# Chunked attention and two feed-forward layers: sums on GpSimd, decode order, side-work edges and rotating output banks

## The chip, the cores and the metric

One core of a Trainium2 chip. It has TensorE (PE; matmuls and, beside them, weight loads, PEld), VectorE (DVE), ScalarE (ACT), GpSimd (POOL) and SyncE (SP), which mostly issues DMAs. Each engine takes its own instructions in order and waits on semaphores. Matmuls write PSUM, here eight banks of 128 x 512 fp32. The metric is the device time of one execution in microseconds.

## The reference

The four weight matrices arrive as float64, the other inputs as fp32. The kernel decodes each weight into an fp32 value from the two 32-bit words of its float64.

```
attention: q, k, v of (8, 8, 576, 64); in each chunk of 64 rows
           softmax(q k^T / 8) v, sums + 1e-9
x = the result as (4608, 512)
h = x @ w_in (512 x 2048);  g = s * relu(h)^2 + b;  y = g @ w_out (2048 x 512)
h2 = y @ w2_in;             g2 = h2 * sigmoid(1.702 h2);  out = g2 @ w2_out
```

## The kernel before, in words

**Tiling.** The 4608 tokens are nine blocks (j) of 512. The 2048 hidden columns are 16 tiles (i) of 128. Every fp32 operand is kept as a rounded part and a rest (hi and lo), and a product is three matmuls: lo x hi, hi x hi, hi x lo. One matmul of 128 x 128 by 128 x 512 fills one bank.

**First layer, blocks 2 to 8 ("steady tiles").** `gemm_in` makes one hidden tile in 12 matmuls into one of two h banks (L487). Then ACT takes Relu (L499) into a buffer r, DVE squares and scales (L500), ACT adds b and rounds to gh (L501), DVE makes the rest gl (L502). Two tiles later `gemm_out` multiplies gh, gl by the second weights into four banks acc0 to acc3 (L562). Blocks 0 and 1 are done at the start, with hidden tiles kept as squares while the weights are still being decoded. Buffers named r, p, qt, kt, pt, wm, wc, ost and so on are all taken from one pool of ten (`tmp`).

**Decoding (`decode`, L116 to L132).** A weight arrives as pairs of 32-bit words (high, low). ACT brings down the low word's upper bits into c (L120), DVE shifts and joins exponent and fraction (L121, L124), GpSimd adds c (L128), ACT squares the high word as fp32 (L129), DVE multiplies by a mask that zeroes tiny values (L131). First weights are then split by ACT (L146) and DVE (L147). Each yield ends a step of the plan; at the start two weights are in flight.

**Second weights and their sums.** While blocks 2 to 8 run, each second weight is decoded and written to DRAM by a GpSimd DMA (L177). `sums` then reads four quarters of two weights back (L190), forms sums and differences for a seven-product block multiplication (Strassen's scheme in Winograd's form) on GpSimd (L193 to L196), rounds them in an ACT copy (L198), takes the rest on GpSimd (L199) and stores both parts by SyncE DMAs (L204). There are 32 such sums, 64 stores of 448 KB.

**Second layer.** Block 0 runs as in the first layer. Blocks 1 to 8 run as four pairs (`Halves`). First phase: eight hidden steps i, each of seven products M1 to M7 (L658) into a bank "x" (acc0 to acc3 by i mod 4), a bank "d" and a bank "b". ACT keeps partial results (L666); `quarter` adds them (L677), takes the sigmoid (L679) and multiplies (L680). M7 and M4 reuse the bank x: M4 may start when quarter 22 has been read by L677, and the bank is free when quarter 21 has been read by L680. Second phase: seven output products in the order M1, M5, M6, M2, M7, M3, M4, each over the eight i and two sides z (L753), with x banks acc2 and acc3; operands are split by ACT and DVE (L730, L731). `result` adds (L769), transposes (L772) and stores four strips by SyncE DMAs (L776).

**Order.** The work is a list of items with planned times (`at`, in units of which a steady tile takes two). It is traced in that order, and a scheduler with a simulated timeline then sets the order on each engine: an instruction whose buffer is not free lets later ones pass. `IN_ORDER` edges bind the order of two instructions of one engine without a semaphore. Items added by `steps_at` are called `step`: attention, decoding, sums and the operands of x.

Of the kernel before, what the change touches and what calls it, by code (L numbers as in the profile page):

```python
# [44 lines left out]
def chunk_attention_two_ffn(ctx, tc, q, k, v, w1_in, w1_out, s, b, w2_in, w2_out, out):  # L45
# [70 lines left out]
    def decode(st, m, c):  # L116

        high, low = st[:, :, 1], st[:, :, 0]
        t = m.bitcast(I32)
        nc.scalar.activation(out=c.bitcast(I32), in_=low.bitcast(U32), func=AF.Copy, scale=2.0 ** -29)  # L120
        nc.vector.tensor_scalar(  # L121
            out=t, in0=high, scalar1=3, scalar2=0x3FFFFFF8, op0=ALU.logical_shift_left, op1=ALU.bitwise_and
        )
        nc.vector.scalar_tensor_tensor(  # L124
            out=t, in0=high, scalar=-0x40000000, in1=t, op0=ALU.bitwise_and, op1=ALU.bitwise_or
        )
        yield
        nc.gpsimd.tensor_tensor(out=t, in0=t, in1=c.bitcast(I32), op=ALU.add)  # L128
        nc.scalar.activation(out=c, in_=high.bitcast(F32), func=AF.Square)  # L129
        yield  # L130
        nc.vector.scalar_tensor_tensor(out=m, in0=c, scalar=TINY * TINY, in1=m, op0=ALU.is_ge, op1=ALU.mult)  # L131
        yield  # L132
# [51 lines left out]
    def sums(kind, i, z):  # L184
# [13 lines left out]
        nc.scalar.activation(out=hi, in_=q[:, 1:8, :], func=AF.Copy)  # L198
# [4 lines left out]
        for part, src in enumerate((hi.bitcast(F32), q[:, 1:8, :])):  # L203
            nc.sync.dma_start(out=to[:, :, part, :], in_=src)  # L204
# [274 lines left out]
    def gemm_in(f, j, i):  # L479
        n = sizes[j]  # L480
        hi, lo = W[f, "wi", i]
        assert done[f, j] == KD
        ps = h_ps.tile([P, n], F32, tag="h", name="h")
# [14 lines left out]
        if f == 0:  # L498
            nc.scalar.activation(out=r, in_=ps, func=AF.Relu)  # L499
            nc.vector.scalar_tensor_tensor(out=r, in0=r, scalar=s_ap, in1=r, op0=ALU.mult, op1=ALU.mult)  # L500
            nc.scalar.activation(out=gh, in_=r, func=AF.Identity, bias=b_ap)  # L501
            nc.vector.scalar_tensor_tensor(  # L502
                out=gl, in0=r, scalar=b_ap, in1=gh.bitcast(F32), op0=ALU.add, op1=ALU.subtract
            )
        else:
            nc.scalar.activation(out=r, in_=ps, func=AF.Sigmoid, scale=1.702)
            nc.vector.tensor_tensor(out=r, in0=ps, in1=r, op=ALU.mult)
            split(gh, gl, r)
# [76 lines left out]
    class Halves:  # L585


        def __init__(self, j, base):
            self.j, self.base = j, base
            self.x, self.w, self.g, self.op, self.ps, self.kept = {}, {}, {}, {}, {}, {}  # L590
# [57 lines left out]
        def first(self, i, m):  # L648
            key = i, BANK[m]
            start = key not in self.ps  # L650
            if start:
                self.bank(key, BANK[m], f"acc{i % KD}")
# [89 lines left out]
        def second(self, n, i):  # L742
            m = OUT_ORDER[n]
            hi, lo = self.op.pop((n, i))
            w = self.wo[n, i // 2]
            for z in range(2):
                key = "out", z, BANK[m]
                start = m in ("M1", "M5", "M2")
                if start and i == 0:
                    self.bank(key, BANK[m], f"acc{HK + z}")  # L750
# [30 lines left out]
        def plan_second(self):  # L781
            self.wo = {}
            base = self.base + 3.5 * HF
            for n, m in enumerate(OUT_ORDER):
                for r in range(HF // 2):
                    at(base + 4 * n + r - 9, self.load_wo, n, r)
                for i in range(HF):
                    t = base + 4 * n + 0.5 * i
                    at(t - 3, self.operand, n, i)
                    at(t, self.second, n, i)  # L790
                done = base + 4 * n + 4.1
                for z in range(2):
                    if m in ("M1", "M5", "M6"):
                        at(done, self.keep_out, z, BANK[m], {"M6": "M16"}.get(m, m))
                    else:
                        at(done, self.result, {"M2": "11", "M7": "22", "M3": "12", "M4": "21"}[m], z)
# [85 lines left out]
    for p in range(NBLK // 2):  # L882
        Halves(1 + 2 * p, NS * (NBLK + 1) + 2 * LAG + 56 * p).plan()
    traced, last = nc.cur_bb.bb.instructions, None
    for t, _, f, a in sorted(ITEMS, key=lambda e: e[:2]):
        n = len(traced)
        f(*a)
        for ins in traced[n:] if t < 2 * NS else ():
# [28 lines left out]
```

## Time and profile before

| | |
|---|---|
| median of 3 runs | 1657.01 us (1655.79 to 1657.5) |
| profiled execution: time, span | 1660.28 us, 1658.5 us |
| PE busy | 1604.2 us (97%) |
| VectorE, ScalarE, GpSimd busy | 1149.3, 747.0, 266.9 us |
| mean granted clock of TensorE | 0.99 |
| HBM traffic | 163 GB/s over the span |

The stages, by the trace: the start with blocks 0 and 1 lasts to about 265 us, blocks 2 to 8 to about 870, block 0 of the second layer to about 1028, and the four pairs take 155 us each. A matmul's end is modelled, so busy time of PE says where it had work, not how well it used the time. "L487 <- ACT r L499" is read as: an instruction of line 487 stood until ACT's instruction of line 499 on buffer r had finished. The number in brackets behind a timeline row is the idle time of the engine just before it.

### The profile page before, as it was taken

The page shows a single profiled execution, that of the slowest core. Times are in us where ns is not written, and L with a number is a line of the kernel's source. Part 1 is how long each engine was busy: PE and PEld are TensorE (multiplying, and loading weights), DVE is VectorE, ACT ScalarE, POOL GpSimd, SP SyncE. Part 2 cuts the span into 40 slices and gives each one's busy share as a digit, 9 for nine tenths or more (in the row PEclk, how much of TensorE's full clock was granted, in tenths as well). Part 3 has the DMA queues.
Part 4 walks back from the last instruction along what each step waited for, and adds up shares of the span by engine and source line. Part 5 has one row for each costly group of instructions (what it writes and reads, how often), then busy time and mean ns, then how long its engine had stood idle before and what let it go on. Part 6 is the DMA issues. An engine that isn't in the chain of part 4 may idle for free.

```text
span 1658.5 us, 24595 instructions
## 1 busy us (share of the span) xinstructions
PE 1604.2 (97%) x8928; PEld 1312.8 (79%) x8928; DVE 1149.3 (69%) x1836; ACT 747.0 (45%) x1258; POOL 266.9 (16%) x294
## 2 busy tenths in 40 slices
PE   6879999999999999999999999999999999999998
PEld 5758887778788878888888888878887888788876
DVE  5876666867687775777757543579568946984685
ACT  3768543333333333333345532456345525653552
POOL 1322101333223223233333000000001000100000
PEclk9889999999999999999999999999999999999999
DMA  9435445656455554646456441676868686767654
GB/s 229 114 102 162 121 132 131 146 132 163 122 141 145 143 136 132 156 128 155 117 160 216 135 135 45 188 239 221 206 195 266 181 221 207 255 183 218 219 192 77
DMA packets 398345, 272.19 MB, mean 164 GB/s; under 512 B 255376, under 2 KB 345488, under 8 KB 398224
## 3 DMA queue, kind: packets, MB, share of 16 engines
q1 hardware_dynamic: 390800, 249.64, 55.0%
q0 software_dynamic: 5120, 16.78, 3.0%
q10 hardware_dynamic: 2304, 4.20, 0.7%
q8 instruction: 71, 1.16, 0.3%
q14 instruction: 50, 0.41, 0.1%
HBM read 209.72 MB, written 60.82 MB: 163 GB/s over the span
## 4 chain that ended last, share of the span: by engine, by line
PE 77%; DVE 8%; DMA 4%; SPq 3%; ACT 3%; issue 2%; POOL 2%; POOLq 0%; DVEq 0%; ACTq 0%
PE acc L562 19%; PE h L487 18%; PE x L658 11%; PE x L753 11%; PE d L658 5%; PE d L753 5%; PE b L658 3%; PE b L753 3%; SPq L235 2%; PE sc L287 1%; PE xT L271 1%; DVE gl L502 1%; DVE r L500 1%; DVE pt L261 1%; ACT gh L501 1%
## 5 line engine op out<-in xcount | busy, mean ns | idle before, releaser
L487 PE MATMUL h<-xh,wi 128*128 128x512 f32 x1280 | 402.7, 396 | 13.5 <-ACT r L517 5.4
L562 PE MATMUL acc<-gh,wo 128*128 128x512 f32 x1152 | 354.8, 394 | 6.0 <-ACT gh L96 3.7
L487 PEld LDWEIGHTS h<-xh,wi 128*128 128x128 f32 x1280 | 240.3, 190 | 66.3 <-ACT r L517 6.3
L562 PEld LDWEIGHTS acc<-gh,wo 128*128 128x128 f32 x1152 | 215.5, 189 | 53.0 <-ACT gh L96 4.1
L487 PE MATMUL h<-xl,wi 128*128 128x512 f32 x640 | 251.2, 394 | 0.0
L562 PE MATMUL acc<-gl,wo 128*128 128x512 f32 x576 | 220.3, 392 | 3.8 <-DVE gl L502 3.8
L501 ACT ACTIVATE gh<-r,sb 128x512 fp32r<-128x512 f32 x112 | 80.9, 723 | 184.4 <-DVE r L500 184.1
L500 DVE SCALAR_TENSOR_TENSOR r<-r,sb 128x512 f32<-128x512 f32 x112 | 103.9, 928 | 64.3 <-ACT r L499 63.8
L502 DVE SCALAR_TENSOR_TENSOR gl<-r,sb,gh 128x512 fp32r<-128x512 f32 x112 | 107.3, 959 | 57.2 <-ACT gh L501 57.1
L487 PEld LDWEIGHTS h<-xl,wi 128*128 128x128 f32 x640 | 121.7, 190 | 25.9
L562 PEld LDWEIGHTS acc<-gl,wo 128*128 128x128 f32 x576 | 108.1, 188 | 28.6 <-DVE gl L502 6.2
L128 POOL TENSOR_TENSOR wm<-wm,wc 128x512 int32<-128x512 int32 x52 | 75.7, 1459 | 338.6 <-DVE wm L124 176.9
L730 ACT ACTIVATE op<-wo 128x512 fp32r<-128x512 f32 x128 | 79.5, 630 | 79.4 <-PE d L753 25.9
L680 DVE TENSOR_TENSOR wo<-wo,r 128x512 f32<-128x512 f32 x96 | 66.0, 691 | 63.0 <-ACT r L679 62.6
L753 PE MATMUL x<-op,wi 128*128 128x512 f32 x432 | 104.4, 389 | 0.0
L658 PE MATMUL x<-xh,wi 128*128 128x512 f32 x320 | 99.5, 391 | 3.1 <-DVE wo L677 3.1
L261 DVE STREAM_TRANSPOSE pt<-p 32x256 f32<-32x256 f32 x224 | 97.7, 436 | 3.9
L597 POOL DMA_DIRECT2D xr<-y x32 | 17.3, 540 | 506.3 <-DVE op L731 262.8
L679 ACT ACTIVATE r<-wo 128x512 f32<-128x512 f32 x96 | 60.8, 633 | 76.8 <-DVE wo L677 76.0
L753 PEld LDWEIGHTS x<-op,wi 128*128 128x128 f32 x432 | 81.1, 188 | 16.9
L731 DVE TENSOR_TENSOR op<-wo,op 128x512 fp32r<-128x512 f32 x128 | 85.2, 680 | 7.4 <-ACT op L730 6.0
L198 ACT ACTIVATE wst<-wst 128x896 fp32r<-128x896 f32 x32 | 30.5, 953 | 128.1 <-POOL wst L196 83.5
(145 smaller groups left out, 2780.1 us busy)
## 6 DMA issues: line engine op xcount, KB each, us to landing
wi<-wo_sums SPq DMA_DIRECT2D x112, 512.0 KB, 3.9
wi<-wi_sums SPq DMA_DIRECT2D x96, 512.0 KB, 3.7
wst<-in_moe_w_out SPq DMA_DIRECT2D x32, 512.0 KB, 4.6
wi_sums<-wst SPq DMA_DIRECT2D x32, 448.0 KB, 3.6
wo_sums<-wst SPq DMA_DIRECT2D x32, 448.0 KB, 3.5
wst<-in_moe_w_in SPq DMA_DIRECT2D x24, 512.0 KB, 5.0
y<-ost SPq DMA_DIRECT2D x36, 256.0 KB, 3.3
xr<-y POOLq DMA_DIRECT2D x32, 256.0 KB, 6.1
```

The costliest lines, as they stand in the source:

```text
L128: nc.gpsimd.tensor_tensor(out=t, in0=t, in1=c.bitcast(I32), op=ALU.add)
L261: nc.vector.transpose(out=pt[r.start + ek * BK:r.start + (ek + 1) * BK, :, eq * BK:(eq + 1) * BK], in_=p[r.start + eq * BK:r.start + (eq + ...
L487: nc.tensor.matmul(out=ps, lhsT=w_[:, kk, :], rhs=x_, start=kk == 0 and a == 0, stop=kk == KD - 1 and a == 2,)
L500: nc.vector.scalar_tensor_tensor(out=r, in0=r, scalar=s_ap, in1=r, op0=ALU.mult, op1=ALU.mult)
L501: nc.scalar.activation(out=gh, in_=r, func=AF.Identity, bias=b_ap)
L502: nc.vector.scalar_tensor_tensor(out=gl, in0=r, scalar=b_ap, in1=gh.bitcast(F32), op0=ALU.add, op1=ALU.subtract)
L562: nc.tensor.matmul(out=acc[m], lhsT=l_, rhs=r_, start=i == 0 and a == 0, stop=i == KF - 1 and a == 2)
L658: nc.tensor.matmul(out=self.ps[key], lhsT=l_, rhs=r_, start=start and k == 0 and a == 0, stop=k == HK - 1 and a == 2, skip_group_check=not ...
L680: nc.vector.tensor_tensor(out=g, in0=h, in1=r, op=ALU.mult)
L730: nc.scalar.activation(out=hi, in_=src, func=AF.Copy)
L731: nc.vector.tensor_tensor(out=lo, in0=src, in1=hi.bitcast(F32), op=ALU.subtract)
L753: nc.tensor.matmul(out=self.ps[key], lhsT=l_, rhs=r_, start=start and i == 0 and a == 0, stop=i == HF - 1 and a == 2, skip_group_check=not ...
```

## The change

- `decode`: Square now writes the staged tile's low words instead of c and comes before the mask; the GpSimd add comes last, after the mask.
- `sums`: the rounding copy moves from ScalarE to GpSimd, and the two stores from SyncE's queue to GpSimd's.
- Steady tiles of the first layer: the four instructions behind a hidden tile are noted with a planned time, and every instruction of a `step` item gets an order-only edge behind the latest noted instruction of its own engine whose time is not later.
- `Halves`: a `turn` of 0, 2, 0, 2 for the four pairs rotates the x banks; the hidden steps begin at acc(turn), the outputs take acc(turn) and acc(turn + 1).
- In the last pair, the last product does side 0 for i = 2 to 7 before side 1, and the result of side 0 is planned right behind it.

```diff
 def decode(st, m, c):
...
         yield
+        square = low.bitcast(F32)
+        nc.scalar.activation(out=square, in_=high.bitcast(F32), func=AF.Square)
+        nc.vector.scalar_tensor_tensor(out=m, in0=square, scalar=TINY * TINY, in1=m, op0=ALU.is_ge, op1=ALU.mult)
+        yield
         nc.gpsimd.tensor_tensor(out=t, in0=t, in1=c.bitcast(I32), op=ALU.add)
-        nc.scalar.activation(out=c, in_=high.bitcast(F32), func=AF.Square)
-        yield
-        nc.vector.scalar_tensor_tensor(out=m, in0=c, scalar=TINY * TINY, in1=m, op0=ALU.is_ge, op1=ALU.mult)
         yield
 def sums(kind, i, z):
...
-        nc.scalar.activation(out=hi, in_=q[:, 1:8, :], func=AF.Copy)
+        nc.gpsimd.tensor_copy(out=hi, in_=q[:, 1:8, :])
...
-            nc.sync.dma_start(out=to[:, :, part, :], in_=src)
+            nc.gpsimd.dma_start(out=to[:, :, part, :], in_=src)
 def gemm_in(f, j, i):
...
+        def steady(d, engine):
+            served.append((NS * j + 2 * i + d, engine, nc.cur_bb.bb.instructions[-1]))
...
             nc.scalar.activation(out=r, in_=ps, func=AF.Relu)
+            steady(2, ACT)
             nc.vector.scalar_tensor_tensor(out=r, in0=r, scalar=s_ap, in1=r, op0=ALU.mult, op1=ALU.mult)
+            steady(2.2, DVE)
             nc.scalar.activation(out=gh, in_=r, func=AF.Identity, bias=b_ap)
+            steady(2.6, ACT)
...
+            steady(2.8, DVE)
 class Halves:
...
+            self.turn = j // 2 * HK % KD
...
-                self.bank(key, BANK[m], f"acc{i % KD}")
+                self.bank(key, BANK[m], f"acc{(self.turn + i) % KD}")
...
-                    self.bank(key, BANK[m], f"acc{HK + z}")
+                    self.bank(key, BANK[m], f"acc{(self.turn + z) % KD}")
...
-                    at(t, self.second, n, i)
-                done = base + 4 * n + 4.1
+                    if self.last and n == len(OUT_ORDER) - 1 and i >= 2:
+                        for z in range(2):
+                            at(base + 4 * n + 1 + 1.5 * z + 0.25 * (i - 2), self.second, n, i, (z,))
+                    else:
+                        at(t, self.second, n, i)
                 for z in range(2):
+                    done = base + 4 * n + (2.6 if self.last and n == len(OUT_ORDER) - 1 and z == 0 else 4.1)
...
     for t, _, f, a in sorted(ITEMS, key=lambda e: e[:2]):
         n = len(traced)
         f(*a)
+        for ins in traced[n:] if f.__name__ == "step" else ():
+            first = next((g for u, e, g in reversed(served) if u <= t and e == ins.engine), None)
+            if first is not None:
+                tc.add_manual_dep(ins, first.name, IN_ORDER, reason="behind the tile before")
```

## Rows read from the trace of the kernel before

**Rows 1.** The page: busy us, share of the span, instructions by engine.
```profile
PE 1604.2 (97%) x8928; PEld 1312.8 (79%) x8928; DVE 1149.3 (69%) x1836; ACT 747.0 (45%) x1258; POOL 266.9 (16%) x294
```

**Rows 2.** Busy us by stage: PE, PEld, DVE, ACT, POOL; clock, DMA share, GB/s.
```profile
40.00:80.00 40.00, 33.86 (x255) 27.38 (x254) 31.97 (x55) 28.27 (x52) 12.42 (x9) 0.87 0.49 117
80.00:120.00 40.00, 30.29 (x260) 23.07 (x261) 32.29 (x54) 26.79 (x51) 11.71 (x8) 0.87 0.31 102
...
1040.00:1195.00 155.00, 152.74 (x673) 125.79 (x672) 113.28 (x180) 76.97 (x134) 4.31 (x8) 1.00 0.72 213
```

**Rows 3.** What PE waited for, whole span: us in total, times, longest.
```profile
PE x L753 <- DVE wo L680: 5.8, 4, 1.5
...
PE x L658 <- DVE wo L677: 3.1, 4, 0.8
```

**Rows 4.** Timeline of PE at the middle of the first pair: start, length, instruction.
```profile
1100.75 0.74 PE L658 MATMUL x<-xh,wi 128*128 128x512 f32 x2 [0.79 <-DVE wo L677]
...
1111.13 0.62 PE L658 MATMUL x<-xh,wi 128*128 128x512 f32 x2
...
1114.12 0.74 PE L753 MATMUL x<-gh,wi 128*128 128x512 f32 x2 [1.47 <-DVE wo L680]
```

**Rows 5.** What PE waited for in 290 to 610 us.
```profile
PE acc L562 <- DVE gl L502: 3.8, 3, 1.4
PE h L487 <- ACT r L499: 2.2, 1, 2.2
PE acc L562 <- ACT gh L501: 1.3, 2, 0.8
```

**Rows 6.** Timeline of ACT: three of the sums' copies and the stand before each.
```profile
337.52 0.95 ACT L198 ACTIVATE wst<-wst 128x896 fp32r<-128x896 f32 x1 [9.94 <-POOL wst L196]
...
422.75 0.95 ACT L198 ACTIVATE wst<-wst 128x896 fp32r<-128x896 f32 x1 [6.60 <-DMA wo_sums<-wst]
...
591.36 0.96 ACT L198 ACTIVATE wst<-wst 128x896 fp32r<-128x896 f32 x1 [5.86 <-DMA wo_sums<-wst]
```

**Rows 7.** Busy us and clock right behind the stand that ends at 337.52.
```profile
338.00:342.00 4.00, 3.00 (x9) 2.45 (x10) 2.23 (x2) 1.67 (x3) 2.96 (x2) 0.76 0.51 131
342.00:346.00 4.00, 4.00 (x16) 3.15 (x15) 0.73 (x1) 0.58 (x1) 1.37 (x3) 0.81 0.92 245
```

**Rows 8.** Timelines of GpSimd and DVE at 338 us, and DVE at 591.
```profile
338.54 2.10 POOL L199 TENSOR_TENSOR wst<-wst 128x896 fp32r<-128x896 f32 x1 [1.06 <-ACT wst L198]
...
338.99 2.21 DVE L500 SCALAR_TENSOR_TENSOR r<-r,sb 128x512 f32<-128x512 f32 x1 [5.90 <-ACT r L499]
...
591.33 0.75 DVE L500 SCALAR_TENSOR_TENSOR r<-r,sb 128x512 f32<-128x512 f32 x1
```

**Rows 9.** Timelines of DVE and of SyncE's queue at the end.
```profile
1650.81 1.40 DVE L772 STREAM_TRANSPOSE ost<-x 128x512 f32<-128x512 f32 x2 [6.60 <-PE x L753]
...
1651.56 4.14 SPq L776 DMA_DIRECT2D out<-ost  x8
```

**Rows 10.** What PE waited for in 240 to 290 us.
```profile
PE h L487 <- ACT r L499: 2.0, 2, 1.2
```

**Rows 11.** What ACT waited for in 40 to 120 us, the rows of L129.
```profile
ACT wc L129 <- POOL wm L128: 4.2, 6, 1.4
ACT wi L129 <- POOL wi L128: 4.1, 6, 2.0
```

**Rows 12.** Groups by line: busy us, mean ns | idle before, what ended it.
```profile
L199 POOL TENSOR_TENSOR wst<-wst 128x896 fp32r<-128x896 f32 x32 | 68.1, 2129 | 50.0 <-ACT wst L198 50.0
...
L129 ACT ACTIVATE wc<-wst 128x512 f32<-128x512 f32 x52 | 34.9, 672 | 33.9 <-POOL wm L128 30.7 <-DMA wst<-in_moe_w_out 3.1
L198 ACT ACTIVATE wst<-wst 128x896 fp32r<-128x896 f32 x32 | 30.5, 953 | 128.1 <-POOL wst L196 83.5 <-DMA wo_sums<-wst 26.0 <-DMA wi_sums<-wst 11.7
...
L597 POOL DMA_DIRECT2D xr<-y x32 | 17.3, 540 | 506.3 <-DVE op L731 262.8 <-ACT r L679 136.5 <-DVE wo L147 39.1
```

**Rows 13.** Busy us of the staged tiles' own instructions, 290 to 910 us.
```profile
290.00:910.00 620.00, 0.00 (x0) 0.00 (x0) 34.47 (x60) 70.49 (x92) 138.90 (x160) 1.00 0.56 146
```

More of the change, by code (lines that the diff above doesn't have):

```diff
@@ L585, in chunk_attention_two_ffn, with __init__ @@
     class Halves:
-        def __init__(self, j, base):
-            self.j, self.base = j, base
+        def __init__(self, j, base, last):
+            self.j, self.base, self.last = j, base, last
+            self.turn = j // 2 * HK % KD
             self.x, self.w, self.g, self.op, self.ps, self.kept = {}, {}, {}, {}, {}, {}
@@ L740, in chunk_attention_two_ffn, with second @@
         n_ops = 0
-        def second(self, n, i):
+        def second(self, n, i, sides=(0, 1)):
             m = OUT_ORDER[n]
-            hi, lo = self.op.pop((n, i))
+            hi, lo = self.op[n, i]
             w = self.wo[n, i // 2]
-            for z in range(2):
+            for z in sides:
                 key = "out", z, BANK[m]
@@ L882, in chunk_attention_two_ffn @@
     for p in range(NBLK // 2):
-        Halves(1 + 2 * p, NS * (NBLK + 1) + 2 * LAG + 56 * p).plan()
+        Halves(1 + 2 * p, NS * (NBLK + 1) + 2 * LAG + 56 * p, p == NBLK // 2 - 1).plan()
+    served = []
     traced, last = nc.cur_bb.bb.instructions, None
```

## The prediction

> **What bounds the kernel now.** I read four views, from wide to narrow. The busy totals come first: TensorE (PE) is busy 97% of the span [rows 1], so a part of the change is worth what it takes out of PE's idle time, or out of the time in which PE has the slow clock. The table by stage shows where these are [rows 2]: at 40 to 120 us PE idles 6.1 and 9.7 us at a mean clock of 0.87; a stage of one pair of blocks (155 us) idles 2.26 us. PE's list of waits then names the causes. In the pair stages they are two, four times each, once per pair: 5.8 us for L680 and 3.1 us for L677 [rows 3]. In the steady tiles, 290 to 610 us, they are six waits of 7.3 us in all, for the instructions of ScalarE (ACT) and VectorE (DVE) that carry a tile from its h bank to its g operand [rows 5]. The timelines of PE and ACT show what stands behind each.
>
> **Banks by pair.** The last M4 product of a pair, from 1111.13, is followed by a gap of 1.47 us for L680, and 0.79 us is lost at 1100.75 for L677 [rows 4]. The output banks are acc2 and acc3, and the last two hidden tiles, i = 6 and i = 7, hold just these. So output side z = 1 cannot start before quarter 21 of i = 7 has been read out of its bank, and z = 0 not before i = 6 is out; PE has nothing else at hand there. With the turn, pair 0 puts its outputs in acc0 and acc1 (last held by i = 4 and 5), pair 1 in acc2 and acc3 while its hidden tiles begin at acc2, and so on. The output matmuls are then free to fill both gaps, since their operands come from quarters of earlier i. At the next pair, i = 0 and 1 take the two banks that were not outputs, and i = 2 meets the old outputs, which is where it met them before. Removed: 5.8 + 3.1 = **8.9 us**. What is late next is PE itself. Bounds: 0 if the order keeps a gap in the same place, 8.9 at most.
>
> **The end.** Now both sides of the last product end within three matmuls: two transposes from 1650.81, then eight output DMAs on SyncE's queue from 1651.56 in 4.14 us (0.52 each), to 1655.70, and the span ends at 1658.5, 2.8 us later [rows 9]. After the change side 0 ends 18 matmuls early, 4.1 us at 152.74 us for 673 [rows 2], and its transpose and four DMAs (0.7 + 2.1 us) lie beside PE. Side 1 still has its transpose (to 1652.21), then four issues (2.07) and 2.8 us: 1657.1. Gain **1.4 us**; bounds 0 (the four early DMAs come late) and 2.1 (four issues).
>
> **GpSimd alone sums.** Each of the 32 sums has an ACT copy, L198, of 0.953 us, before which ACT stood still for 128.1 us in total, 83.5 of them for GpSimd's L196 [rows 12]. ACT works in order, so a tile's Relu or bias queues behind that stand. The longest, 9.94 us, ends at 337.52; others of 6.60 and 5.86 us end at 422.75 and 591.36 [rows 6]. PE waits behind such a stand for 0.8 to 2.2 us at a time [rows 5], and I put all six waits, 7.3 us, down to L198. The 8 us from 338, right behind the longest, also ran at a mean clock of 0.76 and 0.81, that is partly at 1.2 GHz after PE's gap, which costs 4 x 0.24 + 4 x 0.19 = 1.7 us [rows 7]. Sum 9.0 us. I take **7.0 us**: L199 stays on GpSimd, and while it ran (2.10 us from 338.54) the tile's L500 took 2.21 us, where it took 0.75 at 591.33 [rows 8]; a copy by GpSimd adds a second such stretch to each sum, for which I charge 2 us. Bounds 3 and 9.
>
> The Trainium skill ("SBUF — State Buffer", Who interferes with whom) calls the port pair that GpSimd and VectorE share an exclusive lock, under which the later of the two fully blocks; this speaks against the change, and the row of 2.21 us agrees.
>
> What this part adds: 32 copies of 128x896. No row has a one-input pass of this size on GpSimd; the two-input L199 is 2.13 us, half of it is 1.06 [rows 12], and I take 1.6, between the two. Then 64 stores of 448 KB go from SyncE to GpSimd. A DMA of 256 KB holds GpSimd for 0.54 us [rows 12]; a store of the sums has seven times as many rows, shorter ones, so 0.54 to 7 x 0.54 = 3.8 us, and I take 1.0, nearest the row. GpSimd's work on staged tiles is 139 us in 290 to 910 [rows 13]; with 51 of copies, 64 of stores and some 56 of second weights (an add of 512 columns at L199's rate, 1.2 us, and a DMA, 0.54, 32 times) it is 310 of 620 us, and 506 at the upper bounds. So GpSimd stays off the path and I cost it nothing; the cover is that the sums are read only in the pair stages. SyncE loses 64 issues, and loads queued behind them go out sooner; PE's list has no wait for these, so 0.
>
> **Add last in decoding.** Before, the series of one weight is mask bits, GpSimd add, ACT Square, DVE mask, ACT copy, DVE rest; Square waits for the add because it overwrites c. Now Square goes into the staged tile's low words, beside DVE's bit work, and the add comes after the mask. The same passes remain; one Square, 0.67 us [rows 12], leaves the series. In 40 to 120 us ACT stood 4.2 + 4.1 us in front of L129 for the add, twelve times [rows 11]; that goes. But its copy L146 now waits for the add, where it waited for the mask. With two weights in flight and Squares queued behind other ACT work, most of the 0.67 us is lost again. I take **1.0 us**. Bounds: a gain of 8.3 us (all of ACT's stand comes back on PE), and a loss of 6 us (each of the twelve stands grows from its mean of 0.69 us to a whole add of 1.2).
>
> **Side work behind tiles.** These are order-only edges and add no instruction. They bind attention, second weights and sums from block 2 on. An engine must then pass the tile's instruction before that side work; if the tile is late, the side work queues behind it, and the next block's attention waits, with DVE idle 31% of the span to catch up [rows 1]. Since I put the six waits down to L198, these edges find little: 0. The two waits for Relu before 290, 2.0 us [rows 10], lie where attention steps are timed before the first tile of block 2, so they stay; if they vanish, 2.0 us more.
>
> **Sum.** 8.9 + 1.4 + 7.0 + 1.0 = 18.3 us. The profiled execution took 1660.28 us with a span of 1658.5 us: 1642.0 after. The median of the runs is 1657.01, 3.3 us less, so I put it at 1638.7, rounded to **1639 us**.
>
> **Rivals.**
>
> 1. The turn of the banks gives nothing at the turn: another wait (the read of quarter 22, or the operand split) stands where the two were. For it: L677 itself is late at 1100.75 [rows 4]. Against it: output products of side 0 ran up to 1111.13 without a gap, so operands were ready. 1638.7 + 8.9 = 1647.6. Chance 0.10.
>
> 2. Slower: GpSimd's queue becomes the late one. A decode's add follows the second sum's copy, subtraction and two stores (up to 2.1 + 2.1 + 7.6 us), and its two buffers come from the same ten from which each tile takes r. If they come back late, Relu waits. It decides once the hold outgrows 5.86 us, the shortest ACT stand of [rows 6]. 16 such places at 2.2 us, the longest wait of [rows 5]: 35 us, 1638.7 + 35 = 1674. For it: the upper bound of a store. Against it: GpSimd has half its time free. Chance 0.06.
>
> 3. Slower: the lock decides. Copy and subtraction together hold DVE for some 3.7 us at 32 places; at 1.4 us each, the longest wait for gl in [rows 5], this costs 45 us, with no gain from L198: 1638.7 + 7 + 45 = 1691. Against it: PE's waits came behind ACT stands of over 5 us, and these go. Chance 0.04.
>
> 4. The start is ordered anew for the worse: with ACT's copy behind the add, PE's idle time of 40 to 120 us (15.8 us) doubles: 1638.7 + 15.8 = 1654.5. For it: the clock of 0.87 shows how thin PE's supply is there. Against it: the same passes, one fewer in series. Chance 0.06.
>
> **Numbers.** The forecast has 0.74. Its own range: with the lower bounds of three terms and 0.7 of the first (6.2 + 0 + 3 - 6 = 3 us) 1654; with all upper bounds (8.9 + 2.1 + 9 + 8.3 + 2) 1627. Eight times in ten I expect 1629 to 1655, which holds rivals 1 and 4 too. A measurement here tells about 0.2% (3.3 us) from no change, so faster means under 1653.7: forecast and rival 1, 0.84; the same: rival 4, 0.06; slower: rivals 2 and 3, 0.10.
>
> **What would show it.** Right: L677 and L680 gone from PE's waits and pair stages of about 152.7 us; no ACT stand in front of a sum and no PE wait over 1 us in 290 to 610; four DMAs behind the last matmul; ACT's stand for the add moved from L129 to L146. Wrong: a new wait of PE on r, gl or a buffer in 290 to 910, DVE passes of 2 us in pairs, GpSimd stores above 2 us, or more idle time of PE in 40 to 120 us than 15.8 us.

## The result, and the profile after

| | before | after |
|---|---|---|
| median of 14 runs each, on the same chip | 1656.45 us (1654.48 to 1658.17) | 1664.74 us (1659.68 to 1670.54) |
| ratio, 95% interval | | 1.0054 [1.0042, 1.0065] |
| profiled execution: time, span | 1660.28, 1658.5 us | 1665.05, 1663.3 us |

The change makes the kernel 8 to 9 us slower where 18 us less were forecast; the time lies 10 us above the range. The first matmul of each stage, in us from the start of the span, says where (experiment 5 is the changed kernel with one memory doubled; experiment 1 is the kernel before with the turn of the banks alone, so up to the pairs it runs what before runs):

| | before | experiment 1 | after | experiment 5 |
|---|---|---|---|---|
| block 2, first hidden tile | 207.7 | 209.2 | 207.8 | 208.0 |
| block 3 | 365.3 | 364.2 | 358.7 | 356.9 |
| block 4 | 464.1 | 462.9 | 455.1 | 453.3 |
| block 5 | 560.6 | 559.3 | 560.8 | 550.2 |
| second layer, block 0 | 938.0 | 934.2 | 938.1 | 925.0 |
| first pair, first product of a bank x | 1035.7 | 1031.9 | 1035.8 | 1022.7 |
| end of the span | 1658.5 | 1660.4 | 1663.3 | 1651.7 |

The profiled execution of before is 3.8 us above the median of its runs, and above all 14 of them. These 3.8 us lie ahead of the pairs: experiments 1 and 2, whose engines run the same instructions in the same order up to there, both reach the first pair at 1031.9. Against experiment 1 the changed kernel is 7.8 us ahead at block 4, 1.5 us behind at block 5 and 3.9 us behind at the first pair; from there on it loses 4.7 us more against before. These are two separate losses, 8.6 us together, where the medians differ by 8.3.

By this table blocks 2 to 8 last to 938 us and block 0 of the second layer to 1036 us; the 870 and 1028 us in the section on the time before are too early.

Lines have moved in the changed kernel: L687 to L692 are the old L675 to L680, L765 is L753, L670 is L658, L678 is L666, L492 and L571 are L487 and L562, and in the first layer L504, L506, L508, L510 are Relu, square, gh, gl (L499 to L502). In decoding L129 is Square, L132 the add, L147 the split copy; of the sums L199 is the copy, L200 the rest, L205 the store; L178 stores second weights. The first line of the page (busy us, share of the span, instructions) beside [rows 1]: PE's busy time is 3.8 us longer for the same 8928 matmuls, and GpSimd's is 94 us longer.

```profile
PE 1608.0 (97%) x8928; PEld 1313.0 (79%) x8928; DVE 1172.1 (70%) x1836; ACT 719.4 (43%) x1226; POOL 360.6 (22%) x390
```

**The pairs.** What PE waited for, whole span of the changed kernel (us in total, times, longest), beside [rows 3]:

```profile
PE x L670 <- DVE wo L689: 8.7, 4, 2.2
PE acc L571 <- ACT gh L508: 7.1, 6, 3.0
...
PE x L670 <- ACT kept L678: 0.8, 4, 0.2
```

The wait for the old L680 is gone, as forecast. The one for the old L677 (now L689) has grown from 3.1 to 8.7 us, still once per pair: 9.5 us in two groups stand where 8.9 stood. PE's timeline at the middle of the first and the second pair (start, length, instruction, idle time before), beside [rows 4]:

```profile
1104.72 1.75 PE L765 MATMUL x<-op,wi 128*128 128x512 f32 x7
...
1107.67 1.97 PE L765 MATMUL x<-op,wi 128*128 128x512 f32 x8
...
1110.30 0.86 PE L670 MATMUL x<-xo,wi 128*128 128x512 f32 x3
1111.36 0.74 PE L670 MATMUL x<-xh,wi 128*128 128x512 f32 x2 [0.20 <-ACT kept L678]
...
1114.90 0.84 PE L670 MATMUL x<-xo,wi 128*128 128x512 f32 x3
1117.91 0.74 PE L670 MATMUL x<-xh,wi 128*128 128x512 f32 x2 [2.17 <-DVE wo L689]
...
1119.42 1.09 PE L765 MATMUL x<-gh,wi 128*128 128x512 f32 x4
...
1122.17 1.07 PE L765 MATMUL d<-gh,wi 128*128 128x512 f32 x4
...
1273.40 0.73 PE L670 MATMUL x<-xh,wi 128*128 128x512 f32 x2 [2.18 <-DVE wo L689]
...
1275.15 1.91 PE L765 MATMUL x<-gh,wi 128*128 128x512 f32 x4
...
1279.23 1.07 PE L765 MATMUL d<-gh,wi 128*128 128x512 f32 x4
```

From 1111.36 M6, M3, M7 (up to 1114.90) and M4 (1117.91) of i = 7 follow one another with nothing between them. M7 and M4 share the bank x, so M4 stands until DVE has read quarter 22. Before, output matmuls of side 0 stood between the two, among them these twelve:

```profile
1108.41 2.88 PE L753 MATMUL x<-op,wi 128*128 128x512 f32 x12
```

Now they have run earlier, ahead of M7 (1104.72 and 1107.67): the bank for them was free, so the scheduler took them as soon as their operands were there.

The gap is also longer than the read alone needs. DVE's read of a quarter 22 before (i = 6, the gap of 0.79 us) and in the changed kernel (i = 7):

```profile
1100.01 0.69 DVE L677 TENSOR_TENSOR wo<-x,kept 128x512 f32<-128x512 f32 x1 [0.23 <-PE x L658]
```

```profile
1117.17 0.68 DVE L689 TENSOR_TENSOR wo<-x,kept 128x512 f32<-128x512 f32 x1
```

Before, DVE stood idle for M7 and read the bank at once. Now its passes follow one another without a pause, and the read starts 1.4 us after M7's last matmul has ended (1114.90 + 0.84). So of the 2.17 us some 0.8 are the read and 1.4 are DVE's other work ahead of it; no run tests whether another order on DVE would shorten the gap. In the second pair the same four matmuls that took 1.09 us take 1.91. The table by stretch shows why (us, then busy us of PE, PEld, DVE, ACT, POOL; clock, DMA share, GB/s):

```profile
1118.00:1122.00 4.00, 4.00 (x18) 3.27 (x19) 4.00 (x8) 3.54 (x7) 0.13 (x1) 1.00 0.84 288
...
1274.00:1278.00 4.00, 4.00 (x12) 3.14 (x11) 4.00 (x7) 2.72 (x5) 0.55 (x1) 0.57 0.78 257
...
1431.00:1435.00 4.00, 4.00 (x12) 3.13 (x11) 4.00 (x8) 2.79 (x5) 0.55 (x1) 0.57 0.71 241
...
1588.00:1592.00 4.00, 4.00 (x13) 3.13 (x12) 4.00 (x8) 2.32 (x5) 0.00 (x0) 0.58 0.53 164
```

Behind the gap of 2.2 us the granted clock is 0.57 in three of four pairs, that is mostly at 1.2 GHz; behind the gaps of 1.47 and 0.79 us before, it did not fall. From M4's first matmul to the last row shown of each pair (1117.91 to 1122.17, 1273.40 to 1279.23) the same work took 4.26 and 5.83 us: 1.57 us per drop, 4.7 for three. With the 0.6 us of longer gaps and 1.4 us less at the end (run 3 below) this gives 3.9 of the 4.7 us.

**Blocks 4 and 5.** ScalarE's timeline there, then GpSimd's and PE's:

```profile
513.02 0.69 ACT L120 ACTIVATE wc<-wst 128x512 int32<-128x512 uint32 x1 [7.72 <-DMA wst<-in_moe_w_in]
...
524.65 0.68 ACT L120 ACTIVATE wc<-wst 128x512 int32<-128x512 uint32 x1 [3.95 <-DMA wst<-in_moe_w_in]
...
536.62 0.72 ACT L508 ACTIVATE gh<-r,sb 128x512 fp32r<-128x512 f32 x1 [5.84 <-DVE r L506]
```

```profile
505.47 0.91 POOL L205 DMA_DIRECT2D wo_sums<-wst  x1
...
509.37 0.91 POOL L205 DMA_DIRECT2D wo_sums<-wst  x1 [2.49 <-issue]
...
526.57 0.58 POOL L178 DMA_DIRECT2D w_wi<-wm  x1 [2.49 <-issue]
```

```profile
489.23 1.00 PE L571 MATMUL acc<-gh,wo 128*128 128x512 f32 x2 [1.85 <-ACT gh L508]
...
537.39 1.22 PE L571 MATMUL acc<-gh,wo 128*128 128x512 f32 x2 [2.96 <-ACT gh L508]
```

The groups of the sums' copy and rest on GpSimd (busy us, mean ns, then idle before), beside [rows 12]:

```profile
L200 POOL TENSOR_TENSOR wst<-wst 128x896 fp32r<-128x896 f32 x32 | 73.5, 2298 | 1.3
...
L199 POOL CAST wst<-wst 128x896 fp32r<-128x896 f32 x32 | 34.5, 1077 | 60.1 <-DMA wi_sums<-wst 31.5 <-DMA wo_sums<-wst 27.5
```

No copy of a sum is left on ScalarE, and its stands of [rows 6] are gone, but others of the same size stand there: decoding (L120) waits for its load. The load needs one of the three staging buffers. A sum takes two of them, one for the sums and one for their rounded copy, and each stays taken until the store that reads it has landed. SyncE, which issues the loads (L108), waits for that in 290 to 910 us, before and then after:

```profile
SPq L108 <- DMA wo_sums<-wst: 6.2, 8, 1.7
```

```profile
SPq L108 <- DMA wo_sums<-wst: 61.4, 10, 11.4
```

GpSimd issues a store in 0.91 us and then stands ("issue": nothing the profile shows released it) before the next DMA. At 537.39 PE waits for gh, whose DVE pass stood in a run of attention passes, and PE's gap of 2.96 us is the longest of the whole stage. With the gap of 1.85 us and a third of 0.31 PE stands 5.1 us in block 4, and behind the two long ones the clock falls:

```profile
490.00:495.00 5.00, 4.69 (x39) 3.50 (x40) 3.75 (x6) 1.63 (x3) 2.19 (x2) 0.71 0.41 96
...
535.00:540.00 5.00, 2.61 (x6) 1.82 (x7) 3.38 (x6) 1.97 (x4) 4.86 (x6) 0.73 0.07 22
```

By these rows the clock costs some 5 x 0.29 + 5 x 0.27 = 2.8 us. Together that is 7.9 of the 9.3 us by which block 4 is longer than in experiment 1 (105.7 us for 96.4).

**The start and the end.** In 40 to 120 us ACT's stand for the add has moved from L129 [rows 11] to L147 as forecast, 4.3 + 3.4 + 1.4 us for 4.2 + 4.1, and PE is busy 63.9 us of 80, as in [rows 2] (64.2). At the end side 0 is out early: DVE has one last transpose of 0.72 us where two took 1.40 [rows 9]:

```profile
1657.44 0.72 DVE L784 STREAM_TRANSPOSE ost<-x 128x512 f32<-128x512 f32 x1 [1.77 <-PE x L765]
```

### The profile page after: what moved, and what is told of

Same layout as the page of the kernel before. It is cut to its first block, busy times and chain, and to the rows that moved or that the text cites. A ratio compares the mean times of both kernels' runs of the same rounds, so it can differ in the third digit from the quotient of the medians.

```text
span 1663.3 us, 24616 instructions
## 1 busy us (share of the span) xinstructions
PE 1608.0 (97%) x8928; PEld 1313.0 (79%) x8928; DVE 1172.1 (70%) x1836; ACT 719.4 (43%) x1226; POOL 360.6 (22%) x390
## 4 chain that ended last, share of the span: by engine, by line
PE 49%; DVE 3%; ACT 0%; issue 0%
PE x L765 10%; PE x L670 9%; PE acc L571 7%; PE h L492 7%; PE d L765 5%; PE d L670 5%; PE b L765 3%; PE b L670 3%; DVE wo L592 1%; DVE op L743 1%; DVE wo L689 1%; DVE wo L692 0%; PE xT L272 0%; DVE pt L262 0%; ACT op L742 0%
## 5 line engine op out<-in xcount | busy, mean ns | idle before, releaser
L492 PE MATMUL h<-xh,wi 128*128 128x512 f32 x1280 | 401.6, 395 | 14.7 <-ACT r L526 9.4
L571 PE MATMUL acc<-gh,wo 128*128 128x512 f32 x1152 | 356.4, 394 | 7.1 <-ACT gh L508 7.1
L492 PEld LDWEIGHTS h<-xh,wi 128*128 128x128 f32 x1280 | 239.6, 189 | 66.8 <-ACT r L526 10.0
L571 PEld LDWEIGHTS acc<-gh,wo 128*128 128x128 f32 x1152 | 215.5, 189 | 54.6 <-ACT gh L508 9.6
L492 PE MATMUL h<-xl,wi 128*128 128x512 f32 x640 | 250.5, 392 | 0.0
L571 PE MATMUL acc<-gl,wo 128*128 128x512 f32 x576 | 222.5, 394 | 2.1 <-DVE gl L510 1.7
L508 ACT ACTIVATE gh<-r,sb 128x512 fp32r<-128x512 f32 x112 | 81.0, 723 | 221.6 <-DVE r L506 221.2
L506 DVE SCALAR_TENSOR_TENSOR r<-r,sb 128x512 f32<-128x512 f32 x112 | 110.6, 988 | 46.9 <-ACT r L504 46.5
L492 PEld LDWEIGHTS h<-xl,wi 128*128 128x128 f32 x640 | 121.2, 190 | 25.6
L510 DVE SCALAR_TENSOR_TENSOR gl<-r,sb,gh 128x512 fp32r<-128x512 f32 x112 | 104.8, 935 | 47.0 <-ACT gh L508 46.9
L571 PEld LDWEIGHTS acc<-gl,wo 128*128 128x128 f32 x576 | 108.3, 189 | 28.6 <-DVE gl L510 5.4
L132 POOL TENSOR_TENSOR wm<-wm,wc 128x512 int32<-128x512 int32 x52 | 77.3, 1488 | 199.5 <-DVE wm L130 187.6
L504 ACT ACTIVATE r<-h 128x512 f32<-128x512 f32 x112 | 65.8, 588 | 110.6 <-PE h L492 96.4
L692 DVE TENSOR_TENSOR wo<-wo,r 128x512 f32<-128x512 f32 x96 | 66.3, 691 | 63.3 <-ACT r L691 63.3
L670 PE MATMUL x<-xh,wi 128*128 128x512 f32 x320 | 99.8, 393 | 9.5 <-DVE wo L689 8.7
L765 PE MATMUL x<-op,wi 128*128 128x512 f32 x432 | 105.5, 389 | 0.0
L765 PEld LDWEIGHTS x<-op,wi 128*128 128x128 f32 x432 | 81.1, 188 | 16.8
```

What stands on the lines that cost most here:

```text
L492: nc.tensor.matmul(out=ps, lhsT=w_[:, kk, :], rhs=x_, start=kk == 0 and a == 0, stop=kk == KD - 1 and a == 2,)
L510: nc.vector.scalar_tensor_tensor(out=gl, in0=r, scalar=b_ap, in1=gh.bitcast(F32), op0=ALU.add, op1=ALU.subtract)
L571: nc.tensor.matmul(out=acc[m], lhsT=l_, rhs=r_, start=i == 0 and a == 0, stop=i == KF - 1 and a == 2)
L670: nc.tensor.matmul(out=self.ps[key], lhsT=l_, rhs=r_, start=start and k == 0 and a == 0, stop=k == HK - 1 and a == 2, skip_group_check=not ...
L692: nc.vector.tensor_tensor(out=g, in0=h, in1=r, op=ALU.mult)
L765: nc.tensor.matmul(out=self.ps[key], lhsT=l_, rhs=r_, start=start and i == 0 and a == 0, stop=i == HF - 1 and a == 2, skip_group_check=not ...
```

## The experiments

"Held order" below is this edit, on top of what is named: all matmuls of the first output product (n = 0) get an order-only edge, those of i = 0 behind M7 of i = 6, those of i = 1 to 7 behind M7 of i = 7.

```diff
+            if m == "M7":
+                self.m7[i] = nc.cur_bb.bb.instructions[-1]
...
+            for ins in nc.cur_bb.bb.instructions[old:] if n == 0 else ():
+                tc.add_manual_dep(ins, self.m7[HF - 1 if i else HF - 2].name, IN_ORDER, reason="kept for the turn")
```

All runs, each timed against the kernel before on its chip:

| run | median us | ratio [95%] |
|---|---|---|
| 1 before + turn | 1663.87 | 1.0046 [1.0034, 1.0058] |
| 2 before + turn + held order | 1645.91 | 0.9940 [0.9925, 0.9954] |
| 3 changed, banks as before | 1658.63 | 1.0013 [1.0001, 1.0025] |
| 4 changed + held order | 1649.33 | 0.9953 [0.9938, 0.9968] |
| 5 changed, descriptor memory 2048 | 1652.25 | 0.9976 [0.9966, 0.9985] |
| 6 = 4, descriptor memory 2048 | 1636.33 | 0.9883 [0.9866, 0.9899] |
| 7 = 4, stores on SyncE | 1632.73 | 0.9853 [0.9839, 0.9867] |
| 8 = 7, copy on ScalarE | 1634.36 | 0.9864 [0.9850, 0.9878] |
| 9 = 4, four staging buffers | 1646.39 | 0.9933 [0.9919, 0.9947] |
| 10 = 4 without edges | 1647.16 | 0.9944 [0.9930, 0.9958] |
| 11 = 7 without edges | 1632.04 | 0.9851 [0.9838, 0.9865] |
| 12 = 8 without edges | 1644.55 | 0.9921 [0.9907, 0.9935] |
| 13 = 7, decoding as before | 1638.34 | 0.9887 [0.9873, 0.9900] |

Runs 1 to 4 and 7 to 10 stood on one chip, 6 and 11 to 13 on a second, 5 on a third. Where runs on different chips are compared, the difference of the ratios is given beside that of the medians.

**1. The turn alone.** Only the three lines of `turn` on the kernel before.

> The kernel before with the rotation of the x banks alone; PE's order up to the pairs is that of before. Theory A (free output banks let the scheduler place 16 to 36 output matmuls ahead of their plan, so nothing is left to stand between the last M7 and the last M4 of a pair; one gap of 2.2 us takes the place of 1.47 + 0.79, and the clock falls behind it in most pairs): waits for L680 gone, four waits of about 2.2 us for L677, pair period 155.2 to 157.2 us, total 0 to 8 us slower than before (1.000 to 1.005). Rival B (the turn does what was forecast and the loss comes from the other parts): no PE wait at the turns, 8.9 us faster (0.9946).

It alone makes the kernel 0.46% slower, 7 us, nearly the whole loss. PE's waits and one row of its timeline:

```profile
PE x L659 <- DVE wo L678: 8.7, 4, 2.2
```

```profile
1114.00 0.73 PE L659 MATMUL x<-xh,wi 128*128 128x512 f32 x2 [2.15 <-DVE wo L678]
```

The same wait as in the changed kernel, with the sums and the decoding as before: the turn makes it. Behind it the clock falls to 0.57 or 0.58 over 4 us in three of four pairs, as expected. (L659 and L678 are here the old L658 and L677.)

**2. The turn with the order held.** Nothing is added but order edges.

> As turn_only, with order-only edges that keep the output products of i = 0 behind M7 of i = 6 and all others of the first output behind M7 of i = 7; PE then has 23 output matmuls between the last M7 and the last M4. Theory A: both waits of each pair go, pair period 152.4 to 152.9 us, no clock drop in the pairs, 8 to 9.5 us faster than before (0.9943 to 0.9952). Rival B': the banks' turn itself costs (some other wait at the turn): pair period stays 155 us or more, ratio 1.000 or above.

18 us less than run 1. Of all waits from 1020 us to the end one is left:

```profile
PE x L659 <- DMA wi<-wi_sums: 0.5, 1, 0.5
```

The stretch from the first pair's first x product to the end of the span is 612.0 us long, 622.8 before: 10.8 us less, where the forecast for the banks was 8.9 and 8 to 9.5 was expected of this run. The list of waits puts a gap at less than it costs, as these rows of the kernel before show:

```profile
1098.45 0.62 PE L658 MATMUL x<-xh,wi 128*128 128x512 f32 x2
...
1105.01 0.62 PE L658 MATMUL x<-xh,wi 128*128 128x512 f32 x2
```

The six matmuls of M7 that begin at 1098.45 and the listed 0.79 us last to 1100.75, that is 2.30 us; the next M7, from 1105.01, has its six done in 1.36, when the next matmul starts at 1106.37. So 0.94 us went there, and by [rows 4] 2.99 less 1.36, that is 1.63, at the listed 1.47. Four times both are 10.3 us. So the gap is not the price of a turn; it stands where the matmuls that could fill it have been spent.

**3. The changed kernel with the banks as before.**

```diff
-                self.bank(key, BANK[m], f"acc{(self.turn + i) % KD}")
+                self.bank(key, BANK[m], f"acc{i % KD}")
...
-                    self.bank(key, BANK[m], f"acc{(self.turn + z) % KD}")
+                    self.bank(key, BANK[m], f"acc{HK + z}")
```

> The changed kernel with the banks as before (all other parts of the change stay). Theory A: pairs like those of before (155.2 us, waits 1.47 + 0.79, no clock drop), so 5 to 7 us faster than the changed kernel and within 3 us of before: ratio 0.998 to 1.002. Rival B (the loss of the changed kernel is in the steady tiles, through GpSimd's sums or the edges): still slower than before, 1.003 to 1.006.

The old two waits are back at their old sizes:

```profile
PE x L765 <- DVE wo L692: 5.8, 4, 1.5
PE x L670 <- DVE wo L689: 3.1, 4, 0.8
```

The clock stays at 1.00 behind them in all four pairs. From the first pair to the end it takes 621.4 us for 622.8, by which the new end is worth 1.4 us (with the turn it is 1.0 us, the changed kernel against run 1, and 2.2 us, run 4 against run 2). Yet the time stays 0.13% above that of before: the sums, the decoding and the edges together cost some 3.5 us, where a gain of 8.0 was forecast. This run reaches the first pair at 1035.4, 3.5 us after run 1. Turn (+0.46%) and the rest (+0.13%) add up to the whole (+0.54%).

**4. The changed kernel with the order held.**

> The changed kernel with the same order-only edges on the first output product as turn_hold. Theory A: pair period 152.4 to 152.9 us, 14 to 16 us faster than the changed kernel; against before 8 to 12 us faster (0.9928 to 0.9952). Rival B: no better than before, 0.999 or above.

15 us less than the changed kernel (17 by the ratios), and 7.3 us under the kernel before, a little short of the 8 to 12 expected. What is left of the loss lies in 290 to 910 us: PE waits 6.4 us for gh and 1.8 for gl there.

**5 and 6. Room for GpSimd's descriptors.** The memory that the kernel sets aside for the descriptors of the DMAs that GpSimd issues is doubled; the order of the instructions on every engine stays the same. Run 6 does it on run 4, run 5 on the changed kernel itself.

```diff
-    nc = bacc.Bacc("TRN2", target_bir_lowering=False, num_devices=1, dynamic_dma_scratch_size=1024)
+    nc = bacc.Bacc("TRN2", target_bir_lowering=False, num_devices=1, dynamic_dma_scratch_size=2048)
```

> after_hold with twice the room for the descriptors of GpSimd's own DMAs (2048 in place of 1024 bytes per partition); the order of all engines is the same, instruction by instruction. Theory R (the second store of a sum stands 2.5 to 3.9 us until the first one's descriptors have been used up; this stand holds the staging buffers and delays the adds): GpSimd's stands without a visible cause before the stores and the second weights' DMAs (113 us in 290 to 910) fall below 30 us, SyncE's stands for the sums' stores below 70 us (115), PE's waits in 290 to 910 from 8 us to under 4: 3 to 10 us faster than after_hold. Rival P (a DMA issued by GpSimd stands whatever its room, or the stores land late): same stands, within 2 us of after_hold.

> The changed kernel as it is, with 2048 instead of 1024 bytes of descriptor memory for the DMAs that GpSimd issues; the order of the instructions on every engine stays. Theory (two separate causes, the emptied waits at the pairs' turns and GpSimd's full descriptor memory): the descriptor half is worth what it was worth beside the held order (1649.3 to 1636.3, so 13 us of ratio .0070), the turn half stays: 1652 to 1655 us, ratio .997 to .9995 of the kernel before; the gap of about 2.2 us before M4's first matmul stays at the pairs, with the drops of the clock behind it. Rival (the descriptor memory does it all, and the gap at the turn is worth little once the rows before it run freely): about 1640 us. Rival (the two hide each other: what the decode gains is waited for at the turn): 1662 us or more.

13.0 us (run 6 against 4; 11.6 by the ratios) and 12.5 us (run 5 against the changed kernel; 12.9 by the ratios). For run 6 that is more than the 3 to 10 us expected; run 5 lies where its first theory had it. The stores' line, L205, in the changed kernel (instructions with min, median and max ns; then the idle time before them and what ended it):

```profile
L205 POOL DMA_DIRECT2D wo_sums<-wst x32: 888/902/927, 336.7 to 921.9; - x32
...
its engine sat idle before it (us, times) until:
  issue: 78.2, 28
```

and in run 5, where no idle time is listed at all:

```profile
L205 POOL DMA_DIRECT2D wo_sums<-wst x32: 877/914/1077, 334.9 to 899.0; - x32
```

The issue itself costs the same; the 28 stands of 2.8 us on average are gone. Gone too are three stands of 9.6 us in all that the view puts down to DVE and a load, and 13 stands of 36.3 us in front of L178. ScalarE's waits for loads in 290 to 910 us, changed kernel and then run 5:

```profile
ACT wc L120 <- DMA wst<-in_moe_w_in: 25.1, 9, 7.7
ACT wc L120 <- DMA wst<-in_moe_w_out: 24.0, 7, 7.1
```

```profile
ACT wc L120 <- DMA wst<-in_moe_w_in: 13.3, 4, 4.5
...
ACT wc L120 <- DMA wst<-in_moe_w_out: 10.6, 6, 4.7
```

Both are about halved, and PE's waits in 290 to 610 us fall from 7.2 us to the 0.6 of the row below, while those at the turn stay as they were (8.7 and 0.8 us):

```profile
PE acc L571 <- DVE gl L510: 0.6, 2, 0.4
```

SyncE's waits for the sums' stores, though, only go from 115.0 us (L108 and L114 together) to 94.1 in run 5 and 93.2 in run 6, where under 70 was expected; that the staging buffers are the way by which GpSimd's stands reach PE is shown by run 9 rather than here.

In run 5 the clock falls behind the turn in all four pairs; the first of them:

```profile
1106.00:1110.00 4.00, 4.00 (x13) 3.12 (x13) 4.00 (x7) 2.00 (x4) 1.09 (x2) 0.64 0.73 258
```

So the two losses are separate and add up.

**7. The stores back on SyncE,** the copy still on GpSimd, order held.

```diff
-            nc.gpsimd.dma_start(out=to[:, :, part, :], in_=src)
+            nc.sync.dma_start(out=to[:, :, part, :], in_=src)
```

> after_hold with the 64 stores of the sums back on SyncE's queue; the rounding copy stays on GpSimd. Theory S: SyncE's stands for the sums' stores to land before a weight's load (115 us in after_hold) fall below 40 us, ACT's stand at L120 falls from 50 us to under 20, PE's waits for gh fall by 3 to 7 us, clock full after 290 us: 3 to 8 us faster than after_hold (0.990 to 0.994). Rival C (the longer chain of three passes on GpSimd, with the copy, holds the buffers): SyncE stands as long, now for L200 on GpSimd, and the time stays within 2 us of after_hold.

16.6 us less than run 4, twice what was expected, and 24 less than the kernel before: with run 11 the fastest measured. Run 6, with the stores on GpSimd but room for them, lies 3.6 us above it (5.0 by the ratios), and the intervals just touch. PE has no idle time and no slow clock in the steady tiles:

```profile
290.00:610.00 320.00, 320.00 (x2165) 263.88 (x2164) 247.76 (x390) 108.29 (x174) 124.47 (x130) 1.00 0.59 146
610.00:910.00 300.00, 300.00 (x1781) 247.76 (x1780) 217.92 (x327) 111.91 (x182) 114.42 (x120) 1.00 0.55 155
```

The Trainium skill ("DMA: Bandwidth & Descriptors", Issuing engine by pattern) gives simple loads and stores to SyncE and calls its path generally the faster one. The traces agree: an issue of 0.55 us and 3.5 us to landing on SyncE before, 0.90 us and 3.9 us on GpSimd after, beside the stands.

**8. The copy back on ScalarE as well.**

> after_hold with the copy of the sums on ACT and the stores on SyncE, as before the change. Theory S: ACT stands over 100 us in front of that copy again, and PE waits 5 to 9 us in 290 to 610 us as before; in all the time of turn_hold less 1 us at the end (ratio 0.993 to 0.995), no better than after_hold by more than 3 us. Rival C (moving the sums was a loss): 4 us or more faster than after_hold (below 0.9928).

Only 1.6 us more than run 7, and the intervals overlap: with the edges in place the copy on ScalarE costs next to nothing. The first theory, that it would bring back the old stands and 0.993 to 0.995, was wrong; the edges had been left out of it, as run 12 shows.

**9. Four staging buffers for three** (and nine tmp buffers for ten, to make room), stores on GpSimd.

```diff
-    tpool = ctx.enter_context(tc.tile_pool(name="tpool", bufs=10))
-    stpool = ctx.enter_context(tc.tile_pool(name="stpool", bufs=3))
+    tpool = ctx.enter_context(tc.tile_pool(name="tpool", bufs=9))
+    stpool = ctx.enter_context(tc.tile_pool(name="stpool", bufs=4))
```

> after_hold with four staging buffers in place of three, and nine of the shared ten buffers, for room. Theory S: a fourth buffer lets the weight's load go out before the stores have landed: SyncE's stand at L108 and L114 for the stores below 30 us, ACT's at L120 below 15, PE's waits for gh below 3 us, 3 to 8 us faster than after_hold. Rival B (r waits for one of the shared buffers): with nine of them PE's waits grow, 3 us or more slower than after_hold.

2.9 us less than run 4, intervals overlapping. Two sizes change at once, and the trace shows where each acts. Up to the first pair the run is 8.5 us ahead of run 4 (1025.1 us for 1033.6). PE's 8.2 us of waits in 290 to 910 us have shrunk to one row:

```profile
PE acc L571 <- ACT gh L508: 1.3, 1, 1.3
```

ScalarE no longer waits for a staged load there, although GpSimd still stands 86 us in front of its stores and SyncE 106.5 us for them to land (under 30 was expected). So with one staging buffer more the same stands do not reach PE: the buffers are their way. From the first pair on the run loses 9.8 us against run 4 (619.7 for 609.9), with three waits of 5.6 us in all on a buffer for kept results, which come from the pool that lost one.

**10, 11, 12. The edges behind tiles.** `add_manual_dep` is replaced by `pass`, in three settings: runs 4, 7 and 8.

> after_hold without the edges that put side work behind the tiles. Theory S (in the steady tiles GpSimd's own stores hold the staging buffers, so the next weight's load goes out late and ACT and DVE stand at L120 and L121 in front of a tile; the edges only choose where side work stands): about as after_hold, within 3 us (ratio to before 0.993 to 0.997), with ACT still standing some 50 us for staged loads. Rival E (the edges themselves make the late tiles, since side work that waits is bound in front of the next tile): PE's waits for gh fall from 7 us to under 2, 4 us or more faster than after_hold (below 0.993).

> h_sp_stores without the edges that bind side work behind tiles. Theory D (of the 12 us that h_sums_back gained over turn_hold outside the pairs, most is the decode order, since ACT no longer stands for the add): within 3 us of h_sp_stores (0.985 to 0.987). Theory E (the edges keep side work that waits from standing in front of a tile): PE waits 4 us or more in 290 to 910, 5 to 12 us slower than h_sp_stores (0.988 to 0.993).

> h_sums_back without the edges: against turn_hold only the decode order and the end of the last pair differ. Theory D: near h_sums_back (0.985 to 0.988). Theory E: near turn_hold less 1 us (0.992 to 0.994), with ACT standing about 100 us in front of the sums' copy as before.

In two settings nothing moves (2.2 and 0.7 us less without edges, the latter 0.3 by the ratios; intervals overlapping). With the copy on ScalarE the edges are worth 10.2 us (run 12 against run 8; 9.4 by the ratios). The copy's group in run 8 and in run 12 (busy us, mean ns, then idle before):

```profile
L199 ACT ACTIVATE wst<-wst 128x896 fp32r<-128x896 f32 x32 | 30.3, 946 | 36.3 <-POOL wst L197 22.3 <-DMA wo_sums<-wst 7.2 <-issue 2.9
```

```profile
L199 ACT ACTIVATE wst<-wst 128x896 fp32r<-128x896 f32 x32 | 30.5, 953 | 121.3 <-POOL wst L197 77.3 <-DMA wo_sums<-wst 28.5 <-DMA wi_sums<-wst 12.3
```

Without edges the stand is that of [rows 12], 128.1 us; with them the copy goes behind the tile's Relu and stands 36.3. Edges and move are two cures for one stand; either is enough.

**13. Decoding in the old order,** otherwise run 7 (the diff of `decode` undone).

> h_sp_stores with the decode order of before (add, Square, mask). Theory D: 5 to 12 us slower than h_sp_stores (0.988 to 0.993). Theory E: within 3 us of h_sp_stores; ACT stands some 20 us for the add in 290 to 910 but PE does not wait for it.

5.6 us more than run 7, by the medians and by the ratios. In its trace block 2 begins 1.8 us later than in run 7 and block 3 4.6 us later; the later blocks take the same time in both. Over all the profiles, the four with the old order reach block 2 at 207.7 to 209.2 us (mean 208.6), the eleven with the new at 206.4 to 208.2 (mean 207.3).

Set against run 2, which decodes in the same way, this run is 6.4 us ahead at the first pair (1025.5 us for 1031.9). It differs there by the copy on GpSimd and the edges, with the stores left on SyncE.

## Why the prediction was wrong, step by step

**Banks by pair** (forecast: 8.9 us less; the turn alone: 7 us more). The reading of the two waits was right: L680's went with the turn. The step that failed is "The output matmuls are then free to fill both gaps, since their operands come from quarters of earlier i." They are free, but being free they do not wait for the gap. Before, the late bank had by accident held the output products of side 0 back to where they covered the read of quarter 22; with a free bank the scheduler brings them forward, and one gap of 2.17 us remains in place of 1.47 + 0.79, 1.4 of it because DVE comes late to the read. I gave the term a lower bound of 0, and rival 1 the form that came true ("another wait stands where the two were") at a price of nothing. Both left out what a longer single gap does to the clock, though [rows 7] had shown such a drop behind a gap. Runs 1 and 2 show the cause and its remedy; with the order held the banks are worth 10.8 us, so the size too was under what the turn can give.

**GpSimd alone sums** (forecast: 7.0 us less). The stand of ScalarE in front of the copy went, the copy took 1.08 us on average (1.6 was charged), a store's issue 0.90 us (1.0 charged). The step that failed is "So GpSimd stays off the path and I cost it nothing". Its sum of busy time was near enough (281.8 us in 290 to 910 us, where 310 was reckoned) and beside the point: between two stores GpSimd stood for room, 78.2 us in all, the sums held their staging buffers the longer, and the decoding's loads came late. That is near rival 2, but for another buffer: not r from the ten, but the staging buffers for ScalarE's L120. It cost about 12 to 13 us (runs 5 and 6). The gain itself was sized well: with the stores left on SyncE the copy and the edges are worth 6.4 us (run 13 against run 2). Run 5, with room for the stores, is 9.2 us ahead of run 1 at the second layer, where 7.0 + 1.0 was forecast.

**Add last in decoding** (forecast: 1.0 us). The stand moved from L129 to L147 as written, and up to block 2 the new order gains 1.3 us on average over the profiles. In all it is worth 5.6 us where nothing else stands in the way (run 13), 2.8 of it inside block 2, while I had looked only at 40 to 120 us: under-sized, inside its bounds.

**The end** (1.4 us): 1.4 measured in run 3. **Side work behind tiles** (0): right where the copy has left ScalarE, by runs 10 and 11 (both with the held order), and for the reason given; run 12 shows what they would have been worth otherwise. **The lock** (rival 3): bringing the copy to ScalarE changed 1.6 us (run 8), so GpSimd's copy costs DVE nothing that decides. The two DVE passes of a tile took 988 + 935 ns on average in the changed kernel, 928 + 959 before; the rival had 1.4 us at each of 32 places.

The sum: up to the first pair 8.0 us less were forecast and 3.9 more measured (against run 1); from there 10.3 less and 4.7 more. With both causes mended run 6 is at 0.9883, where the forecast stood at 0.989. That is in part luck, since the single terms agree less well: the decoding brought more, and so did the banks.

## What to carry to other kernels

A wait on a buffer also sets an order: before it is taken away, ask what the freed instructions covered where they stood, and whether they will still be there; if not, bind them behind the instruction whose latency they are to hide. Price a DMA that is moved to another queue by its issue and by what that queue can hold: a second one right behind it may stand, and the buffer that it reads stays taken for as long. Two edits that cure the same stand are not to be added up.

## What the runs showed of the hardware

A DMA issued by GpSimd needs room for its descriptors: with 1024 bytes set aside, the changed kernel's stores stood 28 times for 78.2 us in all and the DMAs of L178 13 times for 36.3 us, with 2048 not at all. Nothing in the trace names this but the word "issue" in an otherwise idle GpSimd. What gives the room back, and when, no run shows.

Gaps of PE and its clock: behind one of 2.2 us in otherwise full work the granted clock fell in three of four pairs to 0.57 over 4 us, which cost 1.57 us each time; in run 1 it was three of four too, in run 5 four of four. Gaps of 0.79 and 1.47 us, 13 us apart, left it at 1.00 in all four pairs of the kernel before and of run 3. Why the first pair was spared twice is open.
